# A gated convolution and feed-forward kernel: the small Fourier matmuls run as 64x64 quadrants of the matmul array

## The chip, the cores and the metric

The kernel runs on one core of one Trainium2 chip. The metric is the device time of one execution in microseconds (us). Before the change three runs took 212.46, 212.76 and 213.85 us; the median is 212.76 us. The core's engines, as the profile names them, are PE (matmul), PEld (PE's weight loads), DVE (vector), ACT (scalar), POOL (general) and SP, whose queue only issues transfers here.

## The reference

Cut to what matters:

```
xn = layernorm(A_q)
# branch A: a long convolution over 2048 tokens, for 512 channels
k_shift = sum_t shift_k[t] * k delayed by t        # 4 taps
kv = k_shift * v
y  = irfft(rfft(kv padded to 4096) * rfft(ssm_k padded to 4096))[:2048] + kv * ssm_D
s  = xn * y
# branch B: a gated feed-forward, 512 -> 1792 -> 512
g  = silu((gelu(xn @ w_gate) * (xn @ w_up)) @ w_down)
out = A_q + s * g
```

## The kernel before

**Feed-forward.** The 2048 tokens are 16 tiles of 128, in four quarters of 512 tokens. For each quarter `unit(q, m)` runs 14 times: four matmuls for gate, four for up, each 128x128 by 128x512 in bfloat16; ACT reads the gate bank with Gelu (GE, line 1149), DVE multiplies it with the up bank (HT, line 1152). `down(q)` then multiplies HT with Wd, 14 matmuls per token tile.

**Convolution.** The transforms are matmuls too, in two stages. Stage 1 (`stage1`) multiplies the token tiles with F1 and writes the result to a scratch tensor in HBM, ZH for the filter and ZK for kv. Reading ZH or ZK back puts four frequencies of 32 rows each (16 residues, real and imaginary) on the 128 partitions. Stage 2 therefore needs a 128x128 matrix with four 32x32 blocks on its diagonal and zeros elsewhere; it is MT[:, 0, :], and MT[:, 1, :] and MT[:, 2, :] are the matrices of the inverse. Work goes by pairs: pair n (0 to 15) is two tiles of 128 rows by 512 channels, i = 0 and 1, and takes two PSUM banks.

- Filter, `h_stage2(n)`: load BH from ZH, two matmuls (`fwd`, line 1018), ACT copies with a scale (line 1034), store to ZS.
- kv, the loop at line 1063: load HS from ZS (real and imaginary part of the filter's spectrum, repeated on both rows of a frequency) and BK from ZK; two matmuls (`fwd`); the product with the filter; the inverse (`inv`, line 1113); ACT copies to BO; the ACT queue stores to ZI.
- The last step, `y`, loads BI from ZI and multiplies with G1, the transposed F1.

**The product, before.** It is a complex product, so each row needs its partner row as well. For 14 of the 16 pairs (`psum`, line 1066) it is built like this: DVE multiplies PSUM with HS part 0 into HB (lines 1084, 1098); ACT copies PSUM with a sign per row, COLS[:, 2:3], into KB (line 1101); SP issues two transfers that copy KB's odd rows to KS's even rows and the other way round (`swap`, line 1104); DVE multiplies KS with HS part 1 and adds KS to HB. The inverse is then two matmuls with MT[:, 1, :]. For the other two pairs DVE multiplies PSUM with HS part 1 as well, and the inverse is four matmuls: HB with MT[:, 1, :] and KS with MT[:, 2, :], the matrix that also swaps and signs.

**Order.** Nothing is ordered by hand. Every step is a task of a planner (`Sched.add`, `Sched.run`) with an estimated duration, a priority and buffers out of pools; the planner simulates the engines and writes the instructions in the order it found. On the chip each engine then works strictly in that order, with semaphore waits. Three limits matter here: of the eight PSUM banks the Fourier steps may hold three pairs at once (NC_PAIRS, line 29) and the feed-forward four banks (NF_BANKS, line 27), out of one stock; `fwd` of pair n may not come before the inverse of pair n-4 (AHEAD, line 31); and HS, KB, KS, HB and BK have four buffers each, BO two. The planner's price for a matmul of 512 columns is `pe(n)` = n * (512 / 2.4 + 3) ns (line 411).

Of the kernel before, what the change touches and what calls it, by code (L numbers as in the profile page):

```python
# [28 lines left out]
NC_PAIRS = 3  # L29
SMALL = 1.15 * 262144  # L30
AHEAD = int(4.32)
N_SUM = int(14.8)
HS_FROM = int(13.29)
P_ZS = 0.01
P_HS = 0.2
P_BK = -1
P_KS = -0.49
P_XT = 0.25
P_G1 = 1.22
P_KB = 0.27  # L40
P_PI = 1
P_KM = 3.27
P_LN1 = 2.02
P_LN2 = 3.07
P_LN3 = 7.64
# [377 lines left out]
def build_kernel(nc, A_q, A_k, A_v, A_shift_k, A_ssm_k, A_ssm_D, B_w_gate, B_w_up, B_w_down, out):  # L423
    with ExitStack() as es0:
# [119 lines left out]
        R_G1 = [res(f"G1_{t}", G1[:, t, :, :]) for t in range(NT)]  # L544
        R_M = [res("MT", MT[:])]
        R_id = res("ident", ident[:])
        R_cols, R_col1, R_col2 = (res(f"COLS{i}", COLS[:, i:i + 1]) for i in range(3))
        R_st = [res(f"st{t}", stats[:, t, :]) for t in range(NT)]
        R_mv = [res(f"mv{t}", mv[:, t, :]) for t in range(NT)]
        R_nh = res("NHALF", NHALF[:])  # L550
# [24 lines left out]
        R_BH = [res(f"BH{j}", BH[:, j, :, :]) for j in range(4)]  # L575
        R_BK = [res(f"BK{j}", BK[:, j, :, :]) for j in range(4)]
        R_HS = [twins(f"HS{j}", HS[:, j, :, :, :]) for j in range(4)]
        R_KB = [twins(f"KB{j}", KB[:, j, :, :]) for j in range(4)]
        R_KS = [twins(f"KS{j}", KS[:, j, :, :]) for j in range(4)]
        R_HB = [res(f"HB{j}", HB[:, j, :, :]) for j in range(4)]  # L580
        R_BO = [res(f"BO{j}", BO[:, j, :, :]) for j in range(2)]
        R_BI = [res(f"BI{j}", BI[:, j, :, :]) for j in range(8)]
# [50 lines left out]
        def mm(h, o, l, r, st, sp):  # L633
            return h.matmul(o, lhsT=l, rhs=r, start=st, stop=sp)  # L634
# [274 lines left out]
            return S.add([(eng, dur)], lambda e: trk.op(e, fn, r=rr, w=ww), r=r, w=w, prio=prio, **k)  # L909

        q = R_Q32
        bsgn, bphi, bS32, bmsk, bm = B("sgn"), B("phi"), B("s32"), B("msk"), B("m16")
        bq = [B(f"q{i}") for i in range(16)]

        def iota(o, pat, base, rw, w):
# [14 lines left out]
        qop(10, 0, 1, None, ALU.bitwise_and)  # L930
        qop(8, 10, -2048.0, None, ALU.mult)
        qop(9, 10, 2048.0, None, ALU.mult)
        small("DVE", 180.0, lambda h: h.tensor_scalar(COLS[:, 2:3], Q32[:, 10:11], -2.0, 1.0, ALU.mult, ALU.add), [q], [R_col2], [bq[10]], [bsgn])
        small("POOL", 650.0, lambda h: h.tensor_scalar(PHI[:], PHI[:], Q32[:, 4:5], None, ALU.mult), [q, R_PHI], [R_PHI], [bq[4]], [bphi])
        small("POOL", 650.0, lambda h: h.tensor_scalar(MSK[:], S32[:], Q32[:, 6:7], None, ALU.is_equal), [q, R_S32], [R_MSK], [bq[6], bS32], [bmsk])
        for i, mi in enumerate((M16[:, 0:1, :], M16[:, 1:3, :])):
# [81 lines left out]
        def fwd(p, T, R_T, buf):  # L1018
            def f(e):
                s = psl(p)  # L1020
                for i in range(2):
                    trk.op("PE", lambda h, i=i: mm(h, ps(s, i), MT[:, 0, :], T[:, buf.slot, i, :], True, True),
                           r=[*R_M, R_T[buf.slot]], w=[R_ps[s][i]], accum=True)
            return f

        d_bh = [dsem(f"d_bh{j}") for j in range(4)]
        h2_tasks = []

        def h_stage2(n):
            bh, p, a = B(f"bh{n}", pBH), B(f"psf{n}", pC), B(f"hf{n}", pAST["K"])  # L1030
            S.add([("SP", ISSUE)], lambda e, n=n, bh=bh: dma(e, BH[:, bh.slot, :, :], z_pair(ZH, n), d_bh[bh.slot], R_Z["H"], [R_BH[bh.slot]]),
                  r=bZ["H"], w=[bh], prio=0.5, nbytes=SMALL, after=zh_tasks)
            h2_tasks.append(S.add([("PE", pe(2))], fwd(p, BH, R_BH, bh), r=[bMT, bh], w=[p], prio=4.26, lat=200.0, heavy="ACT"))
            op([("ACT", act(1024))], lambda e, h, p=p, a=a: h.activation(ast["K"][a.slot].rearrange("p c d -> p (c d)"), ps(psl(p)), ACTF.Copy, scale=2.0 ** -12),
               r=[p], w=[a], rr=lambda p=p: R_ps[psl(p)], ww=lambda a=a: [R_AST["K"][a.slot]], prio=2.5, after=kshift_tasks[:1])

            def st(e, n=n, a=a):
                dma(e, ZS[n], ast["K"][a.slot], d_ast["K"][a.slot], [R_AST["K"][a.slot]], [R_Z["S"][n]])
            S.add([("SP", ISSUE)], st, r=[a], w=[bZ["S"][n]], prio=P_ZS, nbytes=262144)
# [16 lines left out]


        d_bk = [dsem(f"d_bk{j}") for j in range(4)]
        d_ks = [[dsem(f"d_ks{j}_{h}") for h in range(2)] for j in range(4)]
        d_hs = [[dsem(f"d_hs{j}_{h}") for h in range(2)] for j in range(4)]  # L1060
        d_bo = [dsem(f"d_bo{j}") for j in range(2)]
        t_inv = []
        for n in range(16):
            bk, hs = B(f"bk{n}", pBK), B(f"hs{n}", pHS)
            pk, pi = B(f"psk{n}", pC), B(f"psi{n}", pC)
            psum = n * N_SUM // 16 < (n + 1) * N_SUM // 16
# [12 lines left out]
            S.add([("PE", pe(2))], fwd(pk, BK, R_BK, bk), r=[bMT, bk], w=[pk], prio=5.9, lat=200.0, after=t_inv[n - AHEAD:n - AHEAD + 1] if n >= AHEAD else [])  # L1079
            def flat(T, b, k=None):  # L1080
                return lambda: (T[:, b.slot, :, :] if k is None else T[:, b.slot, k, :, :]).rearrange("p c d -> p (c d)")

            def tt(o, i0, i1, op_, rr, ww, r, w, prio, rate):
                op([("DVE", dve(1024, rate))], lambda e, h: h.tensor_tensor(o(), i0(), i1(), op_), r=r, w=w, rr=rr, ww=ww, prio=prio)  # L1084

            def r_pk(pk=pk, hs=hs):
                return R_ps[psl(pk)] + R_HS[hs.slot]

            def r_ks(ks=ks):
                return R_KS[ks.slot]  # L1090

            def r_hb(hb=hb):
                return [R_HB[hb.slot]]

            def pk_ap(pk=pk):
                return ps(psl(pk))

            tt(flat(HB, hb), pk_ap, flat(HS, hs, 0), ALU.mult, r_pk, r_hb, [pk, hs], [hb], 2.88, 1)
            if psum:

                op([("ACT", act(1024))], lambda e, h, pk=pk, kb=kb: h.activation(KB[:, kb.slot, :, :].rearrange("p c d -> p (c d)"), ps(psl(pk)), ACTF.Copy, scale=COLS[:, 2:3]),  # L1101
                   r=[pk, bsgn], w=[kb], rr=lambda pk=pk: R_ps[psl(pk)] + [R_col2], ww=lambda kb=kb: R_KB[kb.slot], prio=P_KB)

                def swap(e, kb=kb, ks=ks):
                    for h in range(2):
                        dma(e, KS[h::2, ks.slot, :, :], KB[1 - h::2, kb.slot, :, :], d_ks[ks.slot][h], [R_KB[kb.slot][1 - h]], [R_KS[ks.slot][h]])
                S.add([("SP", 2 * ISSUE)], swap, r=[kb], w=[ks], prio=P_KS, nbytes=262144)
                tt(flat(KS, ks), flat(KS, ks), flat(HS, hs, 1), ALU.mult, lambda r_ks=r_ks, hs=hs: r_ks() + R_HS[hs.slot], r_ks, [hs], [ks], P_KM, 2)
                tt(flat(HB, hb), flat(HB, hb), flat(KS, ks), ALU.add, lambda r_ks=r_ks, r_hb=r_hb: r_ks() + r_hb(), r_hb, [ks], [hb], 0.8, 2)
            else:  # L1110
                tt(flat(KS, ks), pk_ap, flat(HS, hs, 1), ALU.mult, r_pk, r_ks, [pk, hs], [ks], 0.9, 1)

            def inv(e, pi=pi, hb=hb, ks=ks, psum=psum):
                s = psl(pi)
                for i in range(2):
                    trk.op("PE", lambda h, i=i: mm(h, ps(s, i), MT[:, 1, :], HB[:, hb.slot, i, :], True, psum), r=[*R_M, R_HB[hb.slot]], w=[R_ps[s][i]], accum=True)
                    if not psum:
                        trk.op("PE", lambda h, i=i: mm(h, ps(s, i), MT[:, 2, :], KS[:, ks.slot, i, :], False, True), r=[*R_M, *R_KS[ks.slot]], w=[R_ps[s][i]], accum=True)
            t_inv.append(S.add([("PE", pe(2 if psum else 4))], inv, r=[bMT, hb] + ([] if psum else [ks]), w=[pi], prio=P_PI, lat=200.0))
# [183 lines left out]
```

## Time and profile before

| what | value |
|---|---|
| median of three runs | 212.76 us (212.46 to 213.85) |
| profiled execution, first to last instruction | 210.6 us; the page gives no other time of this execution |
| granted PE clock | 1.000 throughout |
| PE busy | 200.7 us (95%), 992 matmuls |
| DVE busy | 171.6 us (81%) |
| ACT busy | 131.7 us (63%) |
| transfers | 61.15 MB, mean 290 GB/s |
| the swap transfers KS<-KB | 28 of 128 KB, 4.5 us each from issue to landing |
| PE waiting, total over the span | 6.2 us in the table of waits |

How to read it: a matmul's record is about 379 ns long, but matmuls overlap in the array, so their spacing (not their length) is what they cost, and the share of busy time hides it. A group in the lists is all instructions of one line, engine and tile; line 634 is the helper that issues nearly every matmul and line 1084 the one that issues the vector products. The time of a transfer from issue to landing includes its waiting behind other transfers.

### The profile page before, as it was taken

The page shows a single profiled execution, that of the slowest core. Times are in us where ns is not written, and L with a number is a line of the kernel's source. Part 1 is how long each engine was busy: PE and PEld are TensorE (multiplying, and loading weights), DVE is VectorE, ACT ScalarE, POOL GpSimd, SP SyncE. Part 2 cuts the span into 40 slices and gives each one's busy share as a digit, 9 for nine tenths or more (in the row PEclk, how much of TensorE's full clock was granted, in tenths as well). Part 3 has the DMA queues.
Part 4 walks back from the last instruction along what each step waited for, and adds up shares of the span by engine and source line. Part 5 has one row for each costly group of instructions (what it writes and reads, how often), then busy time and mean ns, then how long its engine had stood idle before and what let it go on. Part 6 is the DMA issues. An engine that isn't in the chain of part 4 may idle for free.

```text
span 210.6 us, 2937 instructions
## 1 busy us (share of the span) xinstructions
PE 200.7 (95%) x992; PEld 93.4 (44%) x992; DVE 171.6 (81%) x267; ACT 131.7 (63%) x166; POOL 17.0 (8%) x40
## 2 busy tenths in 40 slices
PE   7789999999997999999999999999999999999993
PEld 2466444444433444444444443344434444444452
DVE  5998878878899898989625969989789797439993
ACT  2478767777962598987953767766747766251021
POOL 7284000030300000000100000000000000000000
PEclk9999999999999999999999999999999999999999
DMA  5999999999999989989899999999999741577951
GB/s 189 350 355 338 371 395 390 401 417 334 143 231 244 211 287 301 355 281 356 241 349 394 262 324 260 372 399 324 304 359 341 260 174 54 167 280 214 329 208 52
DMA packets 48229, 61.15 MB, mean 290 GB/s; under 512 B 13907, under 2 KB 33239, under 8 KB 48214
## 3 DMA queue, kind: packets, MB, share of 16 engines
q1 hardware_dynamic: 41414, 52.44, 78.2%
q10 hardware_dynamic: 6800, 8.52, 11.9%
q8 instruction: 8, 0.13, 0.2%
q14 instruction: 7, 0.06, 0.1%
HBM read 35.78 MB, written 18.87 MB: 260 GB/s over the span
## 4 chain that ended last, share of the span: by engine, by line
PE 56%; DMA 18%; SPq 12%; DVE 7%; ACT 4%; issue 2%; POOL 1%; ACTq 0%; DVEq 0%
PE psall L634 56%; SPq L610 12%; DMA X<-in_A_q_dram 7%; DMA xnT<-XN 6%; DMA HS<-ZS 5%; DVE HB L1084 2%; ACT KB L1101 2%; ACT BO L630 1%; DVE stats L817 1%; DVE G L1178 1%; POOL mv L827 1%; DVE mv L818 0%; DVE XN L830 0%; DVE KS L1084 0%; ACTq L610 0%
## 5 line engine op out<-in xcount | busy, mean ns | idle before, releaser
L634 PE MATMUL psall<-xnT,Wg 128*128 128x512 bf16 (+1 forms) x232 | 54.6, 372 | 3.2 <-ACT xnT L630 1.7
L634 PE MATMUL psall<-xnT,Wu 128*128 128x512 bf16 (+1 forms) x232 | 55.7, 372 | 0.3 <-DVE HB L1084 0.3
L634 PE MATMUL psall<-Wd,HT 128*128 128x512 bf16 (+1 forms) x238 | 54.1, 367 | 0.2 <-DVE G L1178 0.2
L1149 ACT ACTIVATE GE<-psall 128x512 bf16<-128x512 f32 x56 | 33.0, 597 | 29.8 <-PE psall L634 28.5
L1152 DVE TENSOR_TENSOR HT<-psall,GE 128x512 bf16<-128x512 f32 x56 | 37.8, 686 | 15.7 <-PE psall L634 15.6
L634 PEld LDWEIGHTS psall<-xnT,Wg 128*128 128x128 bf16 x232 | 22.3, 98 | 30.0 <-ACT xnT L630 2.3
L634 PEld LDWEIGHTS psall<-Wd,HT 128*128 128x128 bf16 x238 | 23.2, 98 | 25.8 <-DVE G L1178 0.7
L634 PEld LDWEIGHTS psall<-xnT,Wu 128*128 128x128 bf16 x232 | 22.5, 98 | 26.3 <-DVE HB L1084 1.2
L1084 DVE TENSOR_TENSOR HB<-psall,HS 128x1024 bf16<-128x1024 f32 x16 | 19.4, 1219 | 3.4 <-ACT KB L1101 2.3
L630 ACT ACTIVATE BO<-psall 128x1024 bf16<-128x1024 f32 x16 | 16.3, 1022 | 5.4 <-PE psall L634 5.4
L1101 ACT ACTIVATE KB<-psall,COLS 128x1024 bf16<-128x1024 f32 x14 | 15.3, 1112 | 5.9 <-PE psall L634 5.9
L630 ACT ACTIVATE ASH<-psall 128x1024 bf16<-128x1024 f32 x16 | 16.3, 1021 | 4.0 <-PE psall L634 4.0
L1007 DVE TENSOR_TENSOR KAC<-KAC,KTM 128x2048 bf16<-128x2048 bf16 x12 | 14.6, 1220 | 0.2
L1005 DVE TENSOR_TENSOR KTM<-KK,SKB 128x2048 bf16<-128x2048 bf16 x12 | 14.6, 1218 | 0.0
L827 POOL TENSOR_TENSOR mv<-mv,NHALF 128x4 f32<-128x4 f32 (+1 forms) x5 | 7.0, 1399 | 83.8 <-DVE mv L826 83.8
L1178 DVE SCALAR_TENSOR_TENSOR G<-G,psall 128x512 bf16<-128x512 bf16 x12 | 7.9, 683 | 6.0 <-ACT G L1176 5.9
L1184 ACT ACTIVATE G<-psall 128x512 bf16<-128x512 f32 (+1 forms) x5 | 2.6, 511 | 15.8 <-PE psall L634 15.8
L817 DVE BATCH_NORM_STATS2 stats<-X 128x6 f32<-128x512 bf16 x16 | 10.5, 674 | 1.7 <-DMA X<-in_A_q_dram 1.7
L1084 DVE TENSOR_TENSOR KS<-KS,HS 128x1024 bf16<-128x1024 bf16 x14 | 9.5, 682 | 1.8 <-DMA KS<-KB 1.8
L630 ACT ACTIVATE AST<-psall 128x1024 bf16<-128x1024 f32 x11 | 10.6, 1026 | 0.1
L634 PE MATMUL psall<-HB,MT 128*128 128x512 bf16 x32 | 9.9, 381 | 0.7 <-DVE HB L1084 0.6
L1084 DVE TENSOR_TENSOR HB<-HB,KS 128x1024 bf16<-128x1024 bf16 x14 | 9.7, 691 | 0.5
(81 smaller groups left out, 194.1 us busy)
## 6 DMA issues: line engine op xcount, KB each, us to landing
HS<-ZS SPq DMA_DIRECT2D x32, 256.0 KB, 4.9
ZH<-ASH ACTq DMA_DIRECT2D x16, 256.0 KB, 6.6
BH<-ZH SPq DMA_DIRECT2D x16, 256.0 KB, 4.6
BK<-ZK SPq DMA_DIRECT2D x16, 256.0 KB, 5.3
ZI<-BO ACTq DMA_DIRECT2D x16, 256.0 KB, 4.3
BI<-ZI SPq DMA_DIRECT2D x16, 256.0 KB, 4.8
KS<-KB SPq DMA_DIRECT2D x28, 128.0 KB, 4.5
ZK<-AST SPq DMA_DIRECT2D x11, 256.0 KB, 2.9
```

Source lines behind the costliest of these rows:

```text
L610: trk.dma(eng, lambda e: e.dma_start(out=out_ap, in_=in_ap), sem, r=r, w=w)
L630: return h.activation(o, i, ACTF.Copy)
L634: return h.matmul(o, lhsT=l, rhs=r, start=st, stop=sp)
L817: t_stats[t] = op([("DVE", 670.0)], lambda e, h, t=t: h.bn_stats(stats[:, t, :], X[:, t, :]), r=[bX[q][t % 4]], w=[bst[t]], rr=[R_X[t]], w ...
L827: t_pw = op([("POOL", 800.0)], lambda e, hd, ts=ts, n=n: hd.tensor_tensor(mv[:, ts, 3:4], mv[:, ts, 2:3], NHALF[:, 0:n, :], ALU.pow), r=[b ...
L1005: op([("DVE", dur)], lambda e, h, j=j, m=m: h.tensor_tensor(KTM[:, m.slot, :, :], kk(j), sk(j), ALU.mult), r=need + [bSKB[j], a], w=[m], r ...
L1007: op([("DVE", dur)], lambda e, h, m=m: h.tensor_tensor(KAC[:, a.slot, :, :], KAC[:, a.slot, :, :], KTM[:, m.slot, :, :], ALU.add), r=[m], ...
L1084: op([("DVE", dve(1024, rate))], lambda e, h: h.tensor_tensor(o(), i0(), i1(), op_), r=r, w=w, rr=rr, ww=ww, prio=prio)
L1101: op([("ACT", act(1024))], lambda e, h, pk=pk, kb=kb: h.activation(KB[:, kb.slot, :, :].rearrange("p c d -> p (c d)"), ps(psl(pk)), ACTF.C ...
L1149: op([("ACT", act(512))], lambda e, h: h.activation(GE[:, g.slot, :], bank(pg), ACTF.Gelu_apprx_tanh), r=[pg], w=[g], rr=lambda: R_bank(pg ...
L1152: op([("DVE", dve(512, 1))], lambda e, h: h.tensor_tensor(HT[:, q % 2, m, :], bank(pu), GE[:, g.slot, :], ALU.mult), r=[pu, g], w=[bHT[q][m]],
L1178: op([("DVE", dve(512, 1))], lambda e, h, g=g, pc=pc: h.scalar_tensor_tensor(out=g, in0=g, scalar=1.0, in1=pc(), op0=ALU.add, op1=ALU.mult ...
```

## The change

All matmuls with MT are now issued by a new function, `quads`, as matmuls of 64 rows by 64 columns with an explicit place in the array. The 128x128 matrix has nothing outside its two 64x64 diagonal blocks. So for each half `row` of the partitions and each tile `col` of the pair, one matmul multiplies the 64x64 block of that half with that half of that tile, in the quadrant (64 row, 64 col). Four matmuls of 512 columns take the place of two. The result lies differently: bank `row` holds half `row` of both tiles, tile `col` on partitions 64 col to 64 col + 63. Filter and kv have the same layout, and the inverse, made the same way, turns it back.

The product has one form for all 16 pairs: ACT copies PSUM to KB without a sign, DVE multiplies KB with HS part 0 into HB and with HS part 1 into KS, both from bfloat16 in SBUF, and the inverse is four quadrants with MT[:, 1, :] on HB and four with MT[:, 2, :] on KS. The swap transfers, the addition, the sign column and the case of the two other pairs are gone. The planner gets fixed prices for the two steps, T_FWD and T_INV. Priorities that have nothing left to govern (P_KS, P_KM) are removed, the others stay.

```
+T_FWD = 400.0
+T_INV = 700.0
...
-                for i in range(2):
-                    trk.op("PE", lambda h, i=i: mm(h, ps(s, i), MT[:, 0, :], T[:, buf.slot, i, :], True, True),
-                           r=[*R_M, R_T[buf.slot]], w=[R_ps[s][i]], accum=True)
+                quads(s, [(0, T, R_T[buf.slot], buf.slot)])
             return f
+
+        def quads(s, terms):
+
+            for n, (k, T, rt, slot) in enumerate(terms):
+                for row in range(2):
+                    for col in range(2):
+                        a, b = slice(64 * row, 64 * row + 64), slice(64 * col, 64 * col + 64)
+                        trk.op("PE", lambda h, a=a, b=b, k=k, T=T, slot=slot, row=row, col=col, n=n: h.matmul(
+                            ps(s, row)[b, :], lhsT=MT[a, k, a], rhs=T[a, slot, col, :], start=n == 0, stop=n == len(terms) - 1, tile_position=(64 * row, 64 * col)),
+                            r=[*R_M, rt], w=[R_ps[s][row]], accum=True)
...
-            h2_tasks.append(S.add([("PE", pe(2))], fwd(p, BH, R_BH, bh), r=[bMT, bh], w=[p], prio=4.26, lat=200.0, heavy="ACT"))
+            h2_tasks.append(S.add([("PE", T_FWD)], fwd(p, BH, R_BH, bh), r=[bMT, bh], w=[p], prio=4.26, lat=200.0, heavy="ACT"))
...
-            tt(flat(HB, hb), pk_ap, flat(HS, hs, 0), ALU.mult, r_pk, r_hb, [pk, hs], [hb], 2.88, 1)
-            if psum:
...
-                tt(flat(KS, ks), flat(KS, ks), flat(HS, hs, 1), ALU.mult, lambda r_ks=r_ks, hs=hs: r_ks() + R_HS[hs.slot], r_ks, [hs], [ks], P_KM, 2)
-                tt(flat(HB, hb), flat(HB, hb), flat(KS, ks), ALU.add, lambda r_ks=r_ks, r_hb=r_hb: r_ks() + r_hb(), r_hb, [ks], [hb], 0.8, 2)
-            else:
-                tt(flat(KS, ks), pk_ap, flat(HS, hs, 1), ALU.mult, r_pk, r_ks, [pk, hs], [ks], 0.9, 1)
...
+            op([("ACT", act(1024))], lambda e, h, pk=pk, kb=kb: copy(e, h, flat(KB, kb), ps(psl(pk))),
+               r=[pk], w=[kb], rr=lambda pk=pk: R_ps[psl(pk)], ww=lambda kb=kb: [R_KB[kb.slot]], prio=P_KB)
+            for k, o, T, R_o in ((0, hb, HB, R_HB), (1, ks, KS, R_KS)):
+                op([("DVE", dve(1024, 2))], lambda e, h, k=k, o=o, T=T, kb=kb, hs=hs: h.tensor_tensor(flat(T, o), flat(KB, kb), flat(HS, hs, k), ALU.mult),
+                   r=[kb, hs], w=[o], rr=lambda kb=kb, hs=hs: [R_KB[kb.slot]] + R_HS[hs.slot], ww=lambda o=o, R_o=R_o: [R_o[o.slot]], prio=0.9)
...
+            def inv(e, pi=pi, hb=hb, ks=ks):
+                quads(psl(pi), [(1, HB, R_HB[hb.slot], hb.slot), (2, KS, R_KS[ks.slot], ks.slot)])
+            t_inv.append(S.add([("PE", T_INV)], inv, r=[bMT, hb, ks], w=[pi], prio=P_PI, lat=200.0))
```

Since prices and tasks changed, the planner finds another order. In the new program the matmuls with MT stand in 31 stretches between other matmuls on PE, where there were 41. Two places: kv's `fwd` of pairs 8 to 11 now come in one piece with the inverses of pairs 8 and 9 straight behind, and the `y` matmuls stand among the gate and up matmuls of the last quarter, where they stood among its down matmuls.

More of the change, by code (lines that the diff above doesn't have):

```diff
@@ L31 @@
 AHEAD = int(4.32)
-N_SUM = int(14.8)
+T_FWD = 400.0
+T_INV = 700.0
 HS_FROM = int(13.29)
@@ L36 @@
 P_BK = -1
-P_KS = -0.49
 P_XT = 0.25
@@ L41 @@
 P_PI = 1
-P_KM = 3.27
 P_LN1 = 2.02
@@ L546, in build_kernel @@
         R_id = res("ident", ident[:])
-        R_cols, R_col1, R_col2 = (res(f"COLS{i}", COLS[:, i:i + 1]) for i in range(3))
+        R_cols, R_col1 = (res(f"COLS{i}", COLS[:, i:i + 1]) for i in range(2))
         R_st = [res(f"st{t}", stats[:, t, :]) for t in range(NT)]
@@ L577, in build_kernel @@
         R_HS = [twins(f"HS{j}", HS[:, j, :, :, :]) for j in range(4)]
-        R_KB = [twins(f"KB{j}", KB[:, j, :, :]) for j in range(4)]
-        R_KS = [twins(f"KS{j}", KS[:, j, :, :]) for j in range(4)]
+        R_KB = [res(f"KB{j}", KB[:, j, :, :]) for j in range(4)]
+        R_KS = [res(f"KS{j}", KS[:, j, :, :]) for j in range(4)]
         R_HB = [res(f"HB{j}", HB[:, j, :, :]) for j in range(4)]
@@ L911, in build_kernel @@
         q = R_Q32
-        bsgn, bphi, bS32, bmsk, bm = B("sgn"), B("phi"), B("s32"), B("msk"), B("m16")
+        bphi, bS32, bmsk, bm = B("phi"), B("s32"), B("msk"), B("m16")
         bq = [B(f"q{i}") for i in range(16)]
@@ L932, in build_kernel @@
         qop(9, 10, 2048.0, None, ALU.mult)
-        small("DVE", 180.0, lambda h: h.tensor_scalar(COLS[:, 2:3], Q32[:, 10:11], -2.0, 1.0, ALU.mult, ALU.add), [q], [R_col2], [bq[10]], [bsgn])
         small("POOL", 650.0, lambda h: h.tensor_scalar(PHI[:], PHI[:], Q32[:, 4:5], None, ALU.mult), [q, R_PHI], [R_PHI], [bq[4]], [bphi])
@@ L1058, in build_kernel @@
         d_bk = [dsem(f"d_bk{j}") for j in range(4)]
-        d_ks = [[dsem(f"d_ks{j}_{h}") for h in range(2)] for j in range(4)]
         d_hs = [[dsem(f"d_hs{j}_{h}") for h in range(2)] for j in range(4)]
@@ L1065, in build_kernel @@
             pk, pi = B(f"psk{n}", pC), B(f"psi{n}", pC)
-            psum = n * N_SUM // 16 < (n + 1) * N_SUM // 16
             kb, ks, hb, bo = B(f"kb{n}", pKB), B(f"ks{n}", pKS), B(f"hb{n}", pHB), B(f"bo{n}", pBO)
@@ L1077, in build_kernel @@
                   r=bZ["K"], w=[bk], prio=P_BK, nbytes=SMALL, after=g1_tasks)
-            S.add([("PE", pe(2))], fwd(pk, BK, R_BK, bk), r=[bMT, bk], w=[pk], prio=5.9, lat=200.0, after=t_inv[n - AHEAD:n - AHEAD + 1] if n >= AHEAD else [])
+            S.add([("PE", T_FWD)], fwd(pk, BK, R_BK, bk), r=[bMT, bk], w=[pk], prio=5.9, lat=200.0, after=t_inv[n - AHEAD:n - AHEAD + 1] if n >= AHEAD else [])
             def flat(T, b, k=None):
-                return lambda: (T[:, b.slot, :, :] if k is None else T[:, b.slot, k, :, :]).rearrange("p c d -> p (c d)")
@@ L1083, in tt @@
[L1083 to L1096, printed above, removed]
-            tt(flat(HB, hb), pk_ap, flat(HS, hs, 0), ALU.mult, r_pk, r_hb, [pk, hs], [hb], 2.88, 1)
@@ L1099, in build_kernel @@
-            if psum:
[L1101 to L1107, printed above, removed]
-                tt(flat(KS, ks), flat(KS, ks), flat(HS, hs, 1), ALU.mult, lambda r_ks=r_ks, hs=hs: r_ks() + R_HS[hs.slot], r_ks, [hs], [ks], P_KM, 2)
-                tt(flat(HB, hb), flat(HB, hb), flat(KS, ks), ALU.add, lambda r_ks=r_ks, r_hb=r_hb: r_ks() + r_hb(), r_hb, [ks], [hb], 0.8, 2)
-            else:
-                tt(flat(KS, ks), pk_ap, flat(HS, hs, 1), ALU.mult, r_pk, r_ks, [pk, hs], [ks], 0.9, 1)
@@ L1113, in inv @@
[L1113 to L1119, printed above, removed]
+                return (T[:, b.slot, :, :] if k is None else T[:, b.slot, k, :, :]).rearrange("p c d -> p (c d)")
```

## The prediction

> **What bounds the kernel now.** I read the page's busy shares first, then the table of stretches, then PE's timeline, because a share of 95% of records that overlap proves little.
>
> ```profile
> PE 200.7 (95%) x992; PEld 93.4 (44%) x992; DVE 171.6 (81%) x267; ACT 131.7 (63%) x166; POOL 17.0 (8%) x40
> ```
>
> ```profile
> 18.50:60.00 41.50, 41.48 (x192) 18.73 (x192) 34.49 (x65) 31.68 (x40) 3.85 (x3) 1.00 1.10 344
> 60.00:115.30 55.30, 53.82 (x249) 24.21 (x249) 45.05 (x61) 39.10 (x50) 1.01 (x1) 1.00 0.96 299
> 115.30:178.00 62.70, 61.19 (x279) 26.13 (x278) 54.72 (x72) 42.65 (x54) 0.00 (x0) 1.00 0.88 292
> 178.00:206.00 28.00, 28.00 (x140) 13.52 (x139) 20.57 (x27) 7.04 (x11) 0.00 (x0) 1.00 0.66 225
> ```
>
> Columns: stretch, length, then busy time of PE, PEld, DVE, ACT, POOL. From 18.5 to 206 us PE is idle for only 0.0 + 1.5 + 1.5 + 0.0 = 3.0 us, at full clock. The 115.3 to 178 stretch is kv's pairs, the part that changes most; DVE is at 54.72 of 62.70 us there, ACT at 42.65. PE's timeline gives the real price:
>
> ```profile
> 126.83 0.60 PE L634 MATMUL psall<-HB,MT 128*128 128x512 bf16 x2 [0.57 <-DVE HB L1084]
> 127.28 1.03 PE L634 MATMUL psall<-xnT,Wu 128*128 128x512 bf16 x4
> ...
> 169.93 1.89 PE L634 MATMUL psall<-xnT,Wg 128*128 128x512 bf16 x8
> 171.66 1.89 PE L634 MATMUL psall<-xnT,Wu 128*128 128x512 bf16 x8
> ```
>
> Columns: start, length, group. Eight matmuls take 171.66 - 169.93 = 1.73 us, so one costs 216 ns although its record is 379 ns. **PE sets the time**: what the change adds to or takes from PE's stream, and what PE waits for, is the answer. DVE's and ACT's savings count only through those waits.
>
> **PE's own stream.** The groups that change, by form:
>
> ```profile
> L634 PE MATMUL psall<-HB,MT 128*128 128x512 bf16 x32 | 9.9, 381 | 0.7 <-DVE HB L1084 0.6
> L634 PE MATMUL psall<-BK,MT 128*128 128x512 bf16 x32 | 9.2, 380 | 0.2
> L634 PE MATMUL psall<-BH,MT 128*128 128x512 bf16 x32 | 9.2, 379 | 0.0
> L634 PE MATMUL psall<-KS,MT 128*128 128x512 bf16 x4 | 1.5, 379 | 0.0
> ```
>
> Removed: 32 + 32 + 32 + 4 = 100 matmuls x 0.216 = 21.6 us. Added: 16 + 16 groups of four quadrants forward and 2 x 16 inverse, 64 groups, 256 quadrant matmuls. The trace has no quadrant. From below, four that stream side by side cost what one matmul of 512 columns costs: 64 x 0.216 = 13.8 us. From above, they run one after another: 256 x 0.216 = 55.3 us. What lies between is the pace at which a weight load and its matmul can be issued; the fastest pairs in the trace are the transposes at the start:
>
> ```profile
> 14.98 1.15 PE L882 MATMUL psall<-ident,Hn 128*128 128x128 bf16 x16
> 15.97 0.60 PE L634 MATMUL psall<-xnT,Wu 128*128 128x256 bf16 x4
> ```
>
> Sixteen in 15.97 - 14.98 = 0.99 us, 62 ns each. Four quadrants at this pace take 0.248 us, just over one matmul. I take that: 64 x 0.248 = 15.9 us.
>
> Then the **changes of the array's form**. The new order has the quadrants in 31 stretches, so 62 changes. Before, neighbouring kinds of matmul follow each other without a gap (the 216 ns above holds across tiles), which speaks for 0. Against it: if the array must be empty, a change costs the record's tail, 379 - 216 = 163 ns, and the restart on an empty array, 127.28 - 126.83 - 2 x 0.216 = 0.018, so 0.18 us; and 163 + 98 = 261 ns if a weight load (98 ns a record) is bare too. One row speaks for 0, one for 0.18; I take the middle, 0.09: 62 x 0.09 = 5.6 us, with 0 and 16.2 us as ends.
>
> The Trainium skill, "TensorEngine Tiling (Array Packing)", section Key Properties, says that changing the tiling mode drains the engine. No run here shows it yet. By it the changes would be 62 x 0.18 = 11.2 us and the stream 5.5 us longer than before; by the rows in which kinds alternate freely it would be 5.7 us shorter. The skill's "TensorE: Matmul & The Clock Gate", section Measured speedup vs the span model, has tiles 4 ns apart, thus about 0.23 us a group by estimate; that would make 64 groups 14.6 us.
>
> Sum of the stream: 15.9 + 5.6 - 21.6 = **-0.1 us**. The halved array work is eaten by issue pace and changes of form.
>
> **DVE and ACT.** Their rows:
>
> ```profile
> L1084 DVE TENSOR_TENSOR HB<-psall,HS 128x1024 bf16<-128x1024 f32 x16 | 19.4, 1219 | 3.4 <-ACT KB L1101 2.3 <-DMA HS<-ZS 1.1
> L1101 ACT ACTIVATE KB<-psall,COLS 128x1024 bf16<-128x1024 f32 x14 | 15.3, 1112 | 5.9 <-PE psall L634 5.9
> L1084 DVE TENSOR_TENSOR KS<-KS,HS 128x1024 bf16<-128x1024 bf16 x14 | 9.5, 682 | 1.8 <-DMA KS<-KB 1.8
> L630 ACT ACTIVATE BO<-psall 128x1024 bf16<-128x1024 f32 x16 | 16.3, 1022 | 5.4 <-PE psall L634 5.4
> ```
>
> DVE loses 19.4 + 9.5 + 9.7 (the additions, 14 x 691) + 2.4 (two products from PSUM) = 41.0 us and gets 32 x 0.682 = 21.8: 19.2 us less, worth nothing by itself since PE is the bound. ACT gets 16 x 1.022 = 16.4 for 15.3: 1.1 us more. The 28 swaps (3.7 of 61 MB, 4.5 us each to land) go; the SP queue holds 28 issues less, and what stands behind, HS and BK loads, comes no later. HS loads stay 32; with four buffers and pairs taken in fours, HS of pair n+4 is asked for when KS of pair n is done, 3 x 1.36 = 4.1 us before its burst ends, and needs 4.9 us; the HT products between bursts (0.686 each, 3 to 5) cover it, but barely for pairs 8 to 11. The sign column's 0.15 us was hidden. The end (last down matmuls, Silu, two products, store) is as before.
>
> **PE's waits.** What kv's pairs cost PE in waiting before is the 1.5 us of its stretch. All of that could go, since the swap is gone. But the new order puts pairs together, and per pair ACT owes KB and BO, 2.04 us, DVE 1.36 us, while PE needs only 3 groups, 0.74 us. Take pairs 8 to 11, where four forward steps and two inverses stand in one piece. Three pairs of PSUM are allowed. At the first step those of inverses 6 and 7 are still held until BO; the fourth forward step needs KB 8 done, inverse 8 needs KB 9 done and its products, inverse 9 needs KB 10. ACT's order is Gelu, BO 6, BO 7, KB 8, 9, 10, 11, Gelu. From the end of the Wu before (0): the forward step 8 ends at 0.3, its result is there at 0.5; ACT: KB 8 to 1.5, KB 9 to 2.55, KB 10 to 3.55, KB 11 to 4.6. Products 8 are done at 1.5 + 1.36 = 2.9, products 9 at 4.25. PE ends inverse 9 at about 4.5 and has worked 4 x 0.25 + 2 x 0.5 = 2.0 us: 2.5 us of waiting, and the next Wg waits for ACT again. Pairs 0 to 3 in the same way: KS 3 is done some 0.9 us after PE could use it; 4 to 7: KB 5 and KB 7 stand behind a BO, about 1.5 us; 12 to 15 lie among down matmuls, about 0.5 us. Together 5.4, say 4.5 since a slower quadrant fills part of it, less 1.5: **+3.0 us**. Ends: -1.5 (all cover holds) and +6.
>
> **Sum.** -0.1 + 3.0 = +2.9 us on the profiled 210.6 us, thus 213.5. Around the span lie 212.76 - 210.6 = 2.2 us by the median, which is what I add: **215.7 us**.
>
> **Rivals.**
> - *Even*: the stream is as reckoned, but the waits are no worse (-1.5 to +1): 211.2 to 213.7. For it: 19.2 us less on DVE and no swap on the way. Against it: the burst of pairs 8 to 11.
> - *Faster*: quadrants stream at 0.216 us a group and the form changes for nothing, in all 31 stretches from about 75 us on: -7.8 us, with +1 of waits 206, with +3 208. It decides from 64g + 62s under 16.4 us, that is, with g = 0.216, a change under 0.04 us. For it: no row shows a price of alternation. Against it: the waits are ACT's, and a faster PE only waits longer in the bursts.
> - *Every change drains and reloads bare*: 15.9 + 16.2 - 21.6 = +10.5, with +3 of waits, part of it filled: 224 to 226.
> - *The change doesn't do what it says*: the quadrants go two by two (128 x 0.216 + 5.6 - 21.6 = +11.6, with +3: 227.4), or singly (+33.7, +3 and +5.6: about 255). For it: no row shows two matmuls side by side.
>
> **Chances.** Forecast (214 to 219) 0.32, even 0.21, faster 0.19, drained 0.15, two by two or singly 0.13. A measurement tells about 1% from no change, here 2.1 us. Faster by over that 0.20, within 0.26, slower 0.54. The range leaves out single quadrants and the fullest saving: 207 to 227.5.
>
> **What would show it.** In the changed profile: groups of four quadrants 0.22 to 0.27 us apart inside a stretch; a gap of about 0.09 us at each end; DVE at about 152 us and no KS<-KB; KB at 1.02 us; PE idle of 4 to 6 us in kv's stretch, ended by DVE KS or ACT KB, the largest at pairs 8 to 11. I am wrong if a quadrant group costs 0.4 us or more, if the gaps are nil, or if PE stays fed.

## The result and the profile after

The changed kernel takes 224.39 us, the median of four runs (223.05 to 226.05). The kernel before, run beside it on the same chip, took 212.61 us (212.31 to 213.85). The ratio is **1.055**, with a 95% interval of 1.0487 to 1.0612: about 5.5% slower, where 1.4% had been forecast. The time lies inside the predicted range, 207 to 227.5 us, which was wide enough to hold a gain of nearly 3% as well. Ratios here and below compare fast runs alone: one of the four runs of e2 and two of the seventeen runs of the kernel before that stand beside e1 to e4 were slow. The profiled execution has a span of 221.7 us against 210.6, so 11.1 us have to be found.

First the page's busy shares of the changed kernel (busy time, share of the span, instructions of each engine):

```profile
PE 204.2 (92%) x1148; PEld 87.9 (40%) x1148; DVE 153.2 (69%) x252; ACT 132.2 (60%) x168; POOL 17.0 (8%) x40
```

DVE did lose its work, from 171.6 us to 153.2. But PE's share fell from 95% to 92% over a longer span. Where, is told by the table of stretches, of which the two in the middle are shown (stretch, length, busy time of PE, PEld, DVE, ACT and POOL with the number of instructions, granted PE clock, DMA share, GB/s):

```profile
60.00:115.30 55.30, 50.98 (x263) 20.43 (x262) 42.80 (x59) 35.81 (x47) 1.01 (x1) 0.97 0.89 288
115.30:178.00 62.70, 56.03 (x369) 19.11 (x368) 34.03 (x54) 42.73 (x53) 0.00 (x0) 0.97 0.71 239
```

PE was idle for 1.5 us in each of the two middle stretches before. Now it is idle for 55.30 - 50.98 = 4.3 us in the second and 62.70 - 56.03 = 6.7 us in the third, and the granted clock is no longer 1.00 in either. In the first and the last stretch PE is never idle. The table of waits on PE says whom it waited for (total us, times, longest):

```profile
PE psall L633 <- DVE V L1007: 4.3, 1, 4.3
PE psall L1028 <- ACT BO L629: 3.1, 5, 0.9
PE psall L1028 <- ACT KB L629: 2.4, 5, 0.7
```

None of these three was in the profile before. There the only row that came from kv's pairs was this one:

```profile
PE psall L634 <- DVE HB L1084: 0.9, 2, 0.6
```

The first of the three is a wait in a part of the kernel that the change doesn't touch.

**An account of the 11.1 us.** Busy time hides what a matmul costs, so I took the start of every matmul on PE from 18.5 us on and subtracted what it costs when PE is fed: 216 ns for 512 columns, a quarter of that for a quadrant. A remainder over 0.3 us I call a wait, a smaller one a small gap.

| from 18.5 us on, us | before | after | difference |
|---|---|---|---|
| cost of the matmuls themselves | 184.2 | 176.0 | -8.2 |
| small gaps: slow clock at 65 to 68.7 us | 0 | 1.4 | +1.4 |
| small gaps: all others | 0.9 | 5.8 | +4.9 |
| waits: at 60 to 65 us | 1.8 | 4.5 | +2.7 |
| waits: kv's pairs, 120 to 155 us | 1.6 | 11.9 | +10.3 |
| sum | 188.5 | 199.6 | +11.1 |

The sum agrees with the spans. The stream of matmuls became 3.3 us shorter (-8.2 + 4.9); the rest, +14.4 us, is waiting and the slow clock that follows it. A wait counted in this way is longer than the idle time in the profile, which starts only when the last record has ended. The 11.9 us hold 1.7 us in which PE had work but ran at a slow clock (147.5 to 149.1 us).

### The profile page after: what moved, and what is told of

Read it like the earlier page. It is cut to its first block, busy times and chain, and to the rows that moved or that the text cites. A ratio compares the mean times of both kernels' runs of the same rounds, so it can differ in the third digit from the quotient of the medians.

```text
span 221.7 us, 3186 instructions
## 1 busy us (share of the span) xinstructions
PE 204.2 (92%) x1148; PEld 87.9 (40%) x1148; DVE 153.2 (69%) x252; ACT 132.2 (60%) x168; POOL 17.0 (8%) x40
## 4 chain that ended last, share of the span: by engine, by line
PE 58%; DMA 15%; SPq 11%; DVE 8%; ACT 4%; POOL 2%; issue 1%; ACTq 0%
PE psall L633 52%; SPq L609 11%; DMA X<-in_A_q_dram 8%; DMA ZI<-BO 7%; PE psall L1028 6%; DVE stats L816 2%; ACT BO L629 2%; POOL mv L826 2%; ACT KB L629 1%; DVE XN L829 1%; DVE KAC L1005 1%; DVE KTM L1003 1%; DVE mv L817 1%; DVE V L1007 1%; DVE KAC L999 1%
## 5 line engine op out<-in xcount | busy, mean ns | idle before, releaser
L633 PE MATMUL psall<-xnT,Wg 128*128 128x512 bf16 (+1 forms) x232 | 55.9, 375 | 2.2 <-ACT xnT L629 1.7
L633 PE MATMUL psall<-xnT,Wu 128*128 128x512 bf16 (+1 forms) x232 | 57.1, 377 | 0.7 <-ACT GE L1126 0.7
L633 PE MATMUL psall<-Wd,HT 128*128 128x512 bf16 (+1 forms) x238 | 52.1, 367 | 0.0
L633 PEld LDWEIGHTS psall<-xnT,Wu 128*128 128x128 bf16 x232 | 21.6, 99 | 28.7 <-issue 3.6
L629 ACT ACTIVATE KB<-psall 128x1024 bf16<-128x1024 f32 x16 | 15.7, 1026 | 3.2 <-PE psall L1028 3.2
L1091 DVE TENSOR_TENSOR HB<-KB,HS 128x1024 bf16<-128x1024 bf16 x16 | 11.0, 687 | 8.7 <-ACT KB L629 8.7
L1005 DVE TENSOR_TENSOR KAC<-KAC,KTM 128x2048 bf16<-128x2048 bf16 x12 | 14.6, 1219 | 0.1
L633 PE MATMUL psall<-V,F 128*128 128x512 bf16 x32 | 9.2, 395 | 4.3 <-DVE V L1007 4.3
L1153 ACT ACTIVATE G<-psall 128x512 bf16<-128x512 f32 x12 | 7.1, 596 | 9.3 <-PE psall L633 8.8
L629 ACT ACTIVATE AST<-psall 128x1024 bf16<-128x1024 f32 x10 | 9.9, 1028 | 2.5 <-PE psall L633 2.5
L1091 DVE TENSOR_TENSOR KS<-KB,HS 128x1024 bf16<-128x1024 bf16 x16 | 10.9, 684 | 0.0
L1040 ACT ACTIVATE AST<-psall 128x1024 bf16<-128x1024 f32 x10 | 10.2, 1030 | 0.0
```

What stands on the lines that cost most here:

```text
L629: return h.activation(o, i, ACTF.Copy)
L1005: op([("DVE", dur)], lambda e, h, m=m: h.tensor_tensor(KAC[:, a.slot, :, :], KAC[:, a.slot, :, :], KTM[:, m.slot, :, :], ALU.add), r=[m], ...
L1091: op([("DVE", dve(1024, 2))], lambda e, h, k=k, o=o, T=T, kb=kb, hs=hs: h.tensor_tensor(flat(T, o), flat(KB, kb), flat(HS, hs, k), ALU.mul ...
```

## The experiments

All ratios are to the kernel before, run beside the kernel on the same chip; its median was 213.8 us for the first four kernels below, 212.8 for the next four and 212.7 for the last two.

### Is it the quadrants? e1: the quadrants alone, in the old order

The matmuls with MT become quadrants; the product with its swap, and the order on every engine, stay as before.

```
-                for i in range(2):
-                    trk.op("PE", lambda h, i=i: mm(h, ps(s, i), MT[:, 0, :], T[:, buf.slot, i, :], True, True), ...
+                quads(psl(p), [(0, T, [R_T[buf.slot]], buf.slot)])
...
+                quads(psl(pi), [(1, HB, [R_HB[hb.slot]], hb.slot)] + ([] if psum else [(2, KS, R_KS[ks.slot], ks.slot)]))
```

> The kernel before with the quadrants alone: every engine's order and the product with its swap are the old ones, only the matmuls with MT go as 64x64 quadrants (50 groups of four in 41 stretches in place of 100 whole matmuls). Theory (the quadrants are sound, order and waits cost the time): stream 50 x 0.216 + 41 x 0.2 - 21.6 = -2.6 us by the spacings of the changed kernel's trace, waits as before, 210.0 us (209 to 211.5). Rival (quadrants slow PE, its clock or its neighbours): 213 us or more.

Measured: 213.1 us against 213.8, ratio 0.9977 (0.9943 to 1.0011). I had written the expectations in us, against 212.6; as ratios the theory is 0.983 to 0.995 and the rival 1.002 or more, and the result is neither. There is no loss, so the quadrants themselves are not the cause. There is no gain that can be told from zero either. By the same account PE's matmuls and small gaps became 3.6 us shorter (-11.0 + 7.4) and its waits 4.2 us longer, where I had expected them unchanged. The table of waits of this kernel shows at what:

```profile
PE psall L1029 <- DVE HB L1092: 2.6, 4, 0.9
...
PE psall L634 <- DVE HB L1092: 0.8, 1, 0.8
```

A faster PE waits longer for the product on DVE (HB): 3.4 us in this table, where it was 0.9 before.

### Is it the order? e2: the new order with whole matmuls

The changed kernel with its product and order, but `quads` issues two matmuls of 128x128 per term, as before the change.

```
+                for i in range(2):
+                    trk.op("PE", lambda h, k=k, T=T, slot=slot, i=i, n=n: mm(h, ps(s, i), MT[:, k, :], T[:, slot, i, :], n == 0, n == len(terms) - 1), ...
```

> The changed kernel with its order and its product, but whole 128x128 matmuls in place of the quadrants (two per forward step, four per inverse). Theory (quadrants sound): 128 x 0.216 = 27.7 us in place of 13.8 + 6.3, so 7.5 us more of stream, of which the waits of kv's pairs hide up to half: 228 to 232 us. Rival (quadrants are what is slow): 218 us or less.

Measured: 225.06, 225.53 and 227.55 us against 213.8, ratio 1.0589 (1.0519 to 1.0659). The changed kernel has 1.055 in its own session. So the loss stands without a single quadrant. I had expected 228 to 232 us: in this order the quadrants are worth 0.004, or 0.8 us, which the two intervals don't tell from nothing. That what they save goes into the waits, as in e1, is likely but not shown here. e1 and e2 together put the whole loss on the new order and product.

### The wait at 60 us. e3: the sign column kept

At 60 us the changed kernel issues four gate matmuls and then stage 1 of tokens whose V isn't ready: V is the last of six operations of 1.2 us on DVE and ends at 65.0 us. In the kernel before, sixteen gate and up matmuls start between 60.5 and 63.8 us, and sixteen more behind a short wait:

```profile
60.52 1.89 PE L634 MATMUL psall<-xnT,Wg 128*128 128x512 bf16 x8 [0.39 <-DMA xnT<-XN]
62.25 1.89 PE L634 MATMUL psall<-xnT,Wu 128*128 128x512 bf16 x8
65.22 1.90 PE L634 MATMUL psall<-xnT,Wg 128*128 128x512 bf16 x8 [1.09 <-DVE G L1178]
```

I suspected that the planner had been thrown into another order by the smallest edit of all: the sign column, one DVE operation of 0.15 us at the start, is gone. e3 puts it back, although nothing reads it.

```
+        small("DVE", 180.0, lambda h: h.tensor_scalar(COLS[:, 2:3], Q32[:, 10:11], -2.0, 1.0, ALU.mult, ALU.add), [q], [R_col2], [bq[10]], [bsgn])
```

> The changed kernel with the unused sign column still computed, one DVE instruction of some 0.15 us, which gives the planner back its old order up to the second quarter. Theory (the 4.5 us for which PE waits at 60 us, and the slow clock behind it, are the planner's order alone): 1.7 + 4.5 us go, the old waits of 1.8 us come back, 220 us (218.5 to 221.5), if the order of kv's pairs is no worse. Rival (the wait comes from the change's own work): 223 us or more, with the wait still there.

Measured: 216.84 us, ratio 1.0185 (1.0118 to 1.0251), better than expected (218.5 to 221.5 us): the order of kv's pairs is another one too, and its waits are shorter. One unused operation of 0.15 us makes the kernel 3.5% faster than the change. Its stretches show the same two middle ones nearer to the kernel before and at full clock:

```profile
60.00:115.30 55.30, 54.30 (x291) 21.68 (x289) 45.09 (x61) 39.99 (x52) 1.01 (x1) 1.00 0.95 303
115.30:178.00 62.70, 57.27 (x376) 21.24 (x376) 35.32 (x55) 41.60 (x53) 0.00 (x0) 1.00 0.76 254
```

The wait for V is gone; 5.4 us of idle time in kv's stretch remain. Its waits there sum to 8.7 us in the account (9.84 less 1.16 at 64 us), where the change has 11.9.

### What does PE wait for among kv's pairs? e4, e6 and e7

Behind the waits "ACT BO" in the changed kernel stands another wait. The table of waits on ACT, then the chain of work from 119 to 145 us (start, length, what):

```profile
ACT BO L629 <- DMA ZI<-BO: 3.2, 3, 1.5
```

```profile
119.34 1.03 ACT BO L629
...
120.39 7.41 DMA ZI<-BO
...
127.82 1.03 ACT BO L629
...
134.97 8.33 DMA ZI<-BO
...
143.33 1.02 ACT BO L629
```

BO has two buffers. The copy to BO of one pair waits until an earlier pair has been stored, 7.4 and 8.3 us by this chain, and everything behind it in ACT's queue waits too, KB of the next pairs among it. e4 is the change with four BO buffers (two of them in space that is free by then), the order unchanged. e6 is e3 with the same edit.

```
+        BO2 = at("BO2", [128, 2, 2, DM], BF16, skb_at)
...
-        d_bo = [dsem(f"d_bo{j}") for j in range(2)]
+        d_bo = [dsem(f"d_bo{j}") for j in range(4)]
...
-            op([("ACT", act(1024))], lambda e, h, pi=pi, bo=bo: copy(e, h, BO[:, bo.slot, :, :].rearrange("p c d -> p (c d)"), ps(psl(pi))),
+            op([("ACT", act(1024))], lambda e, h, pi=pi, n=n: copy(e, h, bo_ap[n % 4].rearrange("p c d -> p (c d)"), ps(psl(pi))),
```

> The changed kernel in its own order, with four buffers for BO in place of two; the planner still counts two. Theory A (the wait of kv's pairs is BO waiting for its store to land, 7.4 and 8.3 us in the chain): ACT's 3.2 us of such waiting go and with it 3 to 5 us, 219.5 to 221.5 us. Theory B (ACT's own order of Gelu, BO and KB and the three PSUM pairs, as predicted): no more than 1.5 us, 223 us or more.

Measured: 222.55 us, ratio 1.0415 (1.0364 to 1.0466). Against the change's 1.055 this is 0.0135, or 2.9 us (by the two intervals 1 to 5 us): a little under the 3 us that theory A asked for at least, and more than theory B's 1.5. ACT's waits for the stores are gone, and the waits of kv's pairs in the account fall from 11.9 to 8.8 us. So the store's wait is real, but it is about a quarter of the loss. In its place stands the next one, ACT's KB:

```profile
PE psall L1031 <- ACT KB L632: 3.3, 6, 1.0
...
PE psall L1031 <- ACT BO L632: 1.3, 2, 0.8
```

> The kernel with the sign column kept (ratio 1.0185 to the kernel before) and, in its own order, four buffers for BO. ACT waits 1.8 us there for stores of BO. Theory (these waits cost PE, in any order): ratio 1.008 to 1.014. Rival (only the order with four pairs in one piece suffered from them): 1.017 or more.

Measured: 215.82 us, ratio 1.015 (1.0097 to 1.0203), against 1.0185 of e3. It lies between the two expectations and the intervals overlap; this run decides nothing.

My theory then was that ACT's serial row (Gelu, BO, KB) is what PE waits for, as the prediction had it. e7 takes half of KB from ACT: in e6's order, DVE copies KB of the odd pairs.

```
+                trk.op("DVE" if n % 2 else "ACT", lambda h: copy("DVE" if n % 2 else "ACT", h, flat(KB, kb), ps(psl(pk))), r=R_ps[psl(pk)], w=[R_KB[kb.slot]])
```

> As the kernel with the sign column kept and four buffers for BO, in the same order, but the copies PSUM to KB of the eight odd pairs go on DVE (1.22 us each) and no longer on ACT (1.03 us each). Theory (ACT's serial row of Gelu, BO and KB is what PE waits for in kv's pairs): 1 to 3 us less, ratio 0.998 to 1.006. Rival (the chain per pair or the three PSUM pairs, whoever copies): no gain or up to 2 us more, since DVE's products then stand behind the copies.

Measured: 220.45 us, ratio 1.0352 (1.0294 to 1.0409), 2% slower than e6. I had expected a gain of 1 to 3 us, and the rival at most 2 us of loss; it lost 4.6. ACT had 32.48 us of work in kv's stretch instead of 41.16, and PE waited longer, now for DVE:

```profile
PE psall L1032 <- DVE KB L633: 3.5, 5, 1.4
```

I read this as follows, without having shown it: PE waits for the chain of one pair (forward step, KB, two products, inverse) in an order that gives it too little other work meanwhile, not for the throughput of one engine. DVE's copy takes 1.22 us against ACT's 1.02 and stands in a queue whose order was written without it, so the run shows only that less work on ACT does not help by itself.

### Is there an order in which it pays? e8 and e10

e8 keeps the sign column, gives the planner prices of 350 and 560 for the two steps, lets the Fourier steps hold two pairs of PSUM instead of three and run two pairs ahead instead of four, and multiplies seven of the 16 pairs on DVE straight from PSUM, without KB. The priorities and other constants of the planner (SLACK, HEDGE and the like) were chosen anew with them, so this is another plan as a whole.

```
-NC_PAIRS = 3
+NC_PAIRS = 2
-AHEAD = int(4.32)
-T_FWD = 400.0
-T_INV = 700.0
+AHEAD = 2
+T_FWD = 350.0
+T_INV = 560.0
...
+            if n in (2, 4, 8, 9, 11, 12, 13):
+                for k, o, T, R_o in ((0, hb, HB, R_HB), (1, ks, KS, R_KS)):
+                    op([("DVE", dve(1024, 1))], lambda e, h, k=k, o=o, T=T, pk=pk, hs=hs: h.tensor_tensor(flat(T, o), ps(psl(pk)), flat(HS, hs, k), ALU.mult), ...
```

> The change with another plan: sign column kept, the planner told 350 and 560 ns for the forward and inverse step (the spacings measured in the changed kernel's trace), two PSUM pairs in place of three, the forward step of pair n behind the inverse of pair n-2, seven pairs (2, 4, 8, 9, 11, 12, 13) multiplied by DVE straight from PSUM without KB, and the priorities set anew; 42 stretches of quadrants. Theory (the change is sound and its order was what cost): stream 13.8 + 42 x 0.2 - 21.6 = +0.6 us, waits no more than the old 3.4 us: 210 to 213.5 us, ratio 0.985 to 1.003. Rival (the product over two inverse matrices keeps PE waiting in any order): ratio 1.015 or more.

Measured: **209.9 us** against 212.76, ratio 0.9864 (0.9824 to 0.9904). This is faster than both kernels and agrees with the theory. Its stretch of kv's pairs:

```profile
115.30:178.00 62.70, 62.49 (x405) 22.69 (x406) 43.93 (x57) 39.23 (x51) 0.00 (x0) 1.00 0.76 249
```

PE is idle for 0.2 us of kv's 62.7, at full clock. e10 is this order with whole matmuls (the edit of e2), which prices the quadrants where PE is fed.

> The kernel with the new plan, in the same order, with whole 128x128 matmuls in place of the quadrants. Theory (where PE is kept fed, the quadrants are worth their saved stream): 128 x 0.216 = 27.7 us in place of 13.8 + 42 x 0.2 = 22.2: 5.5 us more than with quadrants, at least 4. Rival (the saved stream turns into waits here too): 2 us more or less.

Measured: 213.78 us, ratio 1.0049 (1.0021 to 1.0077). The quadrants are worth 1.0049 - 0.9864 = 0.0185, or 3.9 us, here; I had expected 5.5 and at least 4. The account agrees: 4.2 us between the two profiled executions, matmuls -13.8 and small gaps +9.3 at 42 stretches of quadrants (0.22 us a stretch), waits +0.3. (The traces of e6 to e12 lack the records of 12 to 16 matmuls whose weight loads they do have; the account counts these at 0.216 us each, as they would pass for gaps or waits otherwise.) Without the quadrants the new plan is no gain: e10 is half a per cent slower than the kernel before. Its order was written for the quadrants' prices, though, and the kernel before was never planned anew in the same way, so what another plan would give the old product is not known.

### Which part of the new plan? e11 and e12

Both are the change with the sign column and the prices 350 and 560, with the change's own product and priorities; e11 has `AHEAD = 2` as well, e12 leaves it at 4.

```
-T_FWD = 400.0
-T_INV = 700.0
+T_FWD = 350.0
+T_INV = 560.0
```

> The kernel with the sign column kept, product and buffers as in the change, the planner told 350 and 560 ns (measured spacings), and the forward step of pair n behind the inverse of pair n-2 in place of n-4. Theory (a piece of three or four pairs is served by ACT and DVE one after the other, some 1.03 + 1.37 us of latency for the first and more for each next, while PE has nothing else it may do; two at a time lie beside gate, up and down matmuls): the waits of kv's pairs fall from about 8 to under 4 us, ratio 0.990 to 1.006. Rival (ACT's and DVE's work per pair is the bound, in any grouping): ratio 1.012 or more.

> As the last, but with the old distance of four pairs: only the two prices are changed against the kernel with the sign column kept. Theory (grouping): waits of kv's pairs stay above 5 us, ratio 1.006 to 1.02, and clearly above the kernel with two pairs. Rival (the wrong prices, not the grouping, made the bad order): ratio no more than 0.005 above the kernel with two pairs.

Measured: e11 211.25 us, ratio 0.9938 (0.9917 to 0.9959); e12 213.28 us, 1.0018 (0.9996 to 1.0041). From e3 to e12 only the two prices differ, and the ratio falls by 0.017; the step to two pairs ahead takes another 0.008. e11 came out within its theory's range (0.990 to 1.006). I had expected e12 either at 1.006 to 1.02 or within 0.005 of e11, and it is neither: both matter, the prices more. The stretch of kv's pairs, in e11 and then in e12:

```profile
115.30:178.00 62.70, 60.72 (x397) 22.23 (x397) 36.68 (x57) 43.60 (x55) 0.00 (x0) 1.00 0.73 237
```

```profile
115.30:178.00 62.70, 59.60 (x388) 21.81 (x390) 36.12 (x57) 43.32 (x54) 0.00 (x0) 1.00 0.77 256
```

By the account e12's waits sum to 6.1 us and e11's to 3.7, against 16.4 of the change and 9.8 of e3, although product, engines and buffers are the same; among kv's pairs they are 4.8 and 2.1 us, against 11.9 and 8.7. So the order alone, with nothing added but the unused sign column, brings the changed kernel from 1.055 to 1.002 and below: the order is the cause of the loss. The prices 350 and 560 are the measured cost, averaged over the change's 31 stretches at 0.2 us each (31 x 0.2 / 48 = 0.13 us a step; 0.216 + 0.13 = 0.35, 2 x 0.216 + 0.13 = 0.56). Whether they help because they are nearer to the truth, or because any other number gives another order and the change's was a bad draw, is open: neighbouring prices weren't tried, and e3 shows that 0.15 us is enough to move the time by 3.5%.

## Why the prediction was wrong

The direction and the limiting engine were right; the size was not. By its own steps:

**What bounds the kernel.** PE, through its stream and its waits. This held: the 11.1 us are found in the starts of PE's matmuls, and where PE was kept fed (e8) the time fell. That 18.4 us less on DVE is worth nothing by itself held too: the kernel that has them is slower.

**PE's stream: -0.1 predicted, -3.3 found.** PE's timeline of the change, behind the last pair:

```profile
154.87 1.04 PE L633 MATMUL psall<-xnT,Wu 128*128 128x512 bf16 x4
155.84 0.41 PE L1028 MATMUL psall<-HB,MT 64*64 64x512 bf16 x4
156.08 0.39 PE L1028 MATMUL psall<-KS,MT 64*64 64x512 bf16 x4
156.30 0.39 PE L1028 MATMUL psall<-HB,MT 64*64 64x512 bf16 x4
156.51 0.39 PE L1028 MATMUL psall<-KS,MT 64*64 64x512 bf16 x4
156.83 1.04 PE L633 MATMUL psall<-xnT,Wg 128*128 128x512 bf16 x4
```

Inside the stretch, groups of four follow each other at 156.08, 156.30 and 156.51: 0.216 us, exactly the cost of one whole matmul, not 0.248. The pace of the transposes, 62 ns each, was no bound: the four quadrants of a group start 3 to 4 ns apart and run side by side. These 4 ns, from which the prediction had estimated 0.23 us a group, are there, but they don't add to the spacing of groups. At the ends, the four Wu should be over at 154.87 + 0.86 = 155.73 and the quadrants start at 155.84; from 155.84 to 156.83 is 0.99 us for four groups of 0.216. That is 0.11 + 0.13 us for two changes. Over all changes that no wait covers, 58 in this kernel, I get 0.10 us into the quadrants and 0.11 out of them; I had taken 0.09. In the terms of the sum: groups less removed matmuls -5.7 predicted and -8.2 found, of which the pace explains 64 x 0.032 = 2.0 us and the last 0.5 is mostly what the cut at 18.5 us shifts (it leaves out two more matmuls of the change); the changes +5.6 predicted and +4.9 found as small gaps, since some lie under a wait. The Trainium skill, "TensorEngine Tiling (Array Packing)", section Key Properties, has the drain at a change of mode; these gaps agree that something is paid each time, and it is 0.10 to 0.11 us, not the 0.18 I had estimated for a full drain. Whether the array is empty in between, the records don't show, since they overlap.

**DVE and ACT.** As reckoned: DVE 153.2 us (about 152 predicted), KB 1.03 us (1.02 predicted), no swap. The groups of the change (line, engine, operation, tiles and shape, count, then busy us and mean ns of one, then idle time before and what ended it):

```profile
L629 ACT ACTIVATE KB<-psall 128x1024 bf16<-128x1024 f32 x16 | 15.7, 1026 | 3.2 <-PE psall L1028 3.2
L1091 DVE TENSOR_TENSOR HB<-KB,HS 128x1024 bf16<-128x1024 bf16 x16 | 11.0, 687 | 8.7 <-ACT KB L629 8.7
```

HB fell from 1219 to 687 ns, but DVE now waits 8.7 us for KB: a faster product behind a copy.

**"The sign column's 0.15 us was hidden."** On DVE nothing speaks against it; in the planner it was wrong. e3 shows that taking it out costs 3.5%, with the wait at 60 us:

```profile
65.09 1.03 PE L633 MATMUL psall<-V,F 128*128 128x512 bf16 x2 [4.32 <-DVE V L1007]
65.92 1.91 PE L633 MATMUL psall<-xnT,Wu 128*128 128x512 bf16 x4
```

The order of the changed program was there to be read, and I had followed it only through kv's pairs. The step I left out was to go through the rest of PE's order for every place where a producer has moved, V's stage 1 first of all.

**The failing step: "PE's waits", +3.0 predicted (ends -1.5 and +6), +14.4 found, of which 3.0 is slow clock behind waits.** First the wait at 60 us, priced at nothing: +2.7, and +1.4 for the slow clock behind it. Second, kv's pairs, where I had 5.4 us, booked as 4.5, and there are 11.9. The place was right: the longest row of waits among the pairs stands at the forward steps of pairs 8 to 11, ended by ACT.

```profile
143.06 0.41 PE L1028 MATMUL psall<-BK,MT 64*64 64x512 bf16 x4 [0.40 <-ACT BO L629]
144.40 0.41 PE L1028 MATMUL psall<-BK,MT 64*64 64x512 bf16 x4 [0.93 <-ACT BO L629]
145.32 0.41 PE L1028 MATMUL psall<-BK,MT 64*64 64x512 bf16 x4 [0.50 <-ACT KB L629]
146.23 0.50 PE L1028 MATMUL psall<-BK,MT 64*64 64x512 bf16 x4 [0.51 <-ACT KB L629]
147.15 0.64 PE L1028 MATMUL psall<-HB,MT 64*64 64x512 bf16 x4 [0.42 <-ACT KB L629]
```

From 143.06 on each group of 0.22 us stands 0.9 to 1.3 us from the next, one of ACT's copies apart. I had reckoned 2.5 us there; from 142.5 us, where the Wu before are over, to 147.15 it is 0.56 + 1.27 + 3 x 0.85 = 4.4 us, with another 1.65 us of slow clock in the four groups behind. The two terms that I didn't reckon are the wait of BO for its store (2.9 us over the kernel, e4) and the clock. My row of ACT had BO 6 and BO 7 done 0.5 us after the Wu and KB 8 at 1.5; in the trace the two BO, held back 1.5 and 0.3 us by stores, end 0.5 and 1.85 us after it and KB 8 at 2.8. Pairs 0 to 7, for which I had 2.4 us, show 5.0, three of the six waits ended by BO, two by KB and one by the Gelu behind a BO; pairs 12 to 15, for which I had 0.5, show none. Gelu behind the burst adds 0.85 us. Third, the mechanism behind my numbers, ACT's serial row as the limit, is not confirmed: with half the copies gone from ACT (e7) the kernel is slower. And with the two prices alone changed (e3 to e12) the waits shrink from 9.8 to 6.1 us while the operations stay the same. My reckoning took the order as it was, walked through one piece of it and estimated the other pairs from that; the trace says that an engine's slack in sum is no slack at the place where PE waits.

**The rivals.** *Even* and *faster* were out by the same waits, though the quadrants were as fast as *faster* had it (0.216 us a group). *Every change drains and reloads bare* gave 224 to 226, which is the time that came out, but by a mechanism that is wrong: a change of form costs 0.10 to 0.11 us and not 0.26, and e2 is as slow without any quadrant. *Two by two* is refuted by the 0.216 us. A number that agrees says nothing of its reason.

## What to carry to other kernels

Where a planner writes the order, a changed price or a removed operation of 0.15 us is a new program: go through the new order of the limiting engine from end to end, each matmul with its last producer, before any duration is added up. Sixty-four by sixty-four quadrants do stream four abreast, but each stretch of them costs about 0.2 us more, so they are worth having in few long stretches and where PE isn't kept waiting: 3.9 us in an order that feeds PE (e10 to e8), nothing that can be told from zero in two that don't (e1, e2). Work taken off an engine with slack is no gain until the limiting engine's waits are shown to end there.

## What the hardware showed that was not expected

**Waiting costs twice.** The stretches around the two worst waits of the changed kernel, with the granted clock in the third column from the right:

```profile
65.00:68.40 3.40, 3.31 (x9) 1.24 (x10) 2.95 (x6) 1.02 (x1) 0.00 (x0) 0.57 1.00 201
145.00:149.50 4.50, 3.26 (x26) 0.77 (x27) 4.20 (x7) 3.52 (x5) 0.00 (x0) 0.66 0.83 227
```

After 4.3 us without a matmul the granted clock was 0.57 over the next 3.4 us, with matmuls about 0.42 us apart instead of 0.216. After the chain of waits at pairs 8 to 11, none of which left PE idle for more than 0.93 us, it was 0.66, and the groups of quadrants were 0.43 to 0.49 us apart (147.15 to 148.50). Both figures are means: the trace has the clock at 0.50 for 3.4 us each time, from 64.5 and from 146.4 us, and at 1.00 around them. So a row of short waits was enough here. It isn't always: in e4 a like row at the same pairs, and in e3 single waits of 1.5 us, passed at full clock. The Trainium skill, "TensorE: Matmul & The Clock Gate", section A second HAM failure mode: psum-queue depth-cycling, tells of something of this kind: small idle times between groups of matmuls after which the clock goes down. The second place agrees with it. Together the two cost 1.4 + 1.65 = 3.0 us of the 11.1.

**Quadrants load and run side by side.** Four loads and four matmuls of 64 rows and 64 columns pass in 0.216 us, although the 128x128 transposes at the start, with 128 columns each, do not go below 62 ns a pair. A single load is no shorter (102 to 107 ns a record, against 98 for a whole one); the four start 3 to 4 ns apart.

**At a change of form the weight load comes no earlier than its matmul.** PE's timeline of the changed kernel at the start and at the end of a stretch of quadrants, with the loads (PEld):

```profile
76.94 0.14 PEld L1028 LDWEIGHTS psall<-BH,MT 64*64 64x64 bf16 x8 [0.42 <-issue]
76.94 0.63 PE L1028 MATMUL psall<-BH,MT 64*64 64x512 bf16 x8
77.49 0.55 PEld L633 LDWEIGHTS psall<-xnT,Wu 128*128 128x128 bf16 x4 [0.41 <-issue]
77.50 1.04 PE L633 MATMUL psall<-xnT,Wu 128*128 128x512 bf16 x4
```

Elsewhere in the stream a load's record mostly starts 0.21 us before that of its matmul, while the matmul before is still running; at all 62 changes of this kernel it starts at most 5 ns before. The load's record is 0.10 us long, and so is what a change costs. That the one is the reason for the other is not shown.
